# One tile for a chunk's running products and their reciprocals, so that the keys and the queries are each scaled by one VectorE instruction

## The chip, the core and the metric

The kernel runs on one core of a Trainium2 chip, and the metric is the device time in microseconds. Five engines of the core work side by side, each on its own list of instructions in order: TensorE (PE, matrix products; PEld is its loading of weights), VectorE (DVE), ScalarE (ACT), GpSimd (POOL) and SyncE (SP, which here issues nearly all transfers). An engine waits at an instruction until the semaphores of what it needs are set, and everything behind it on that engine waits too.

## The reference, cut to what matters

A linear attention with a decaying state (4 batches, 8 heads, 768 steps, 48 numbers a head) feeds a gated projection and then a mixture of 8 experts of which each row uses 2.

```python
for t in range(S):
    cur = np.einsum('bhd,bhe->bhde', u[None] * kt, vt)
    y[:, :, t] = np.einsum('bhd,bhde->bhe', rt, state + cur)
    state = wt[:, :, :, None] * state + np.einsum('bhd,bhe->bhde', kt, vt)
...
a = x @ w1
b = x @ w2
h = a * b @ w3
x = h @ w_out
...
# two experts of each row, by noisy logits, weights by a softmax over the two
h = np.maximum(x[mask] @ w1[e], 0.0)
out[mask] += top2_w[mask, k, None] * (h @ w2[e])
```

The changed part is the attention. With w the decay of a step, the product of the decays between two steps s < t is what multiplies k at s and r at t.

## The kernel before, in words

The 3072 rows are cut into 24 chunks of 128 steps (six to a batch). A chunk's steps are ordered around its middle: half of them run outwards to the right, half to the left (HC = 64 steps each). `pre_scan` makes, by one scan on VectorE, the running products of w in both directions for 4 pairs of heads (8 runs of 65 numbers, the first of each a 1). `pre_rec` makes their reciprocals: step 0 on ScalarE (exp of minus the log), step 1 one Newton step in two VectorE instructions. `pre_k` scales the keys, `pre_r` the queries: one half of the steps by a running product, the other half by a reciprocal. The products stand in the tile `fg` (two buffers), the reciprocals in `rc` (one buffer), so each half is an instruction of its own with 256 numbers a lane: two for k (L231, L232), two for r (L237, L238). Signs are settled by a factor of -1 inside the two that read `rc`.

The scaled keys and queries `kt` and `rt` go to TensorE (`at_A`, L263: the scores within a chunk). The bonus term needs u·r·k summed over a head: `pre_u` forms it in the tile `rku` (one buffer) from the chunk's `nrk` (r and k by rows, loaded by `load_rk`, two buffers), on VectorE for chunks 2 to 4 and on GpSimd for all others; `pre_c` sums it on VectorE into `cc`; `pre_d` makes eight diagonal tiles `am` from it on ScalarE, and `at_ov` (L268) lays the masked scores over them. `at_y` (L332) then gives the chunk's output, and `at_kv` (L296) the state.

Around the attention stand 19 steps that multiply w3 by w_out while the weights arrive (their conversion, `cvt` and `flush`, keeps VectorE and ScalarE busy: L166, L168, L173), then 12 groups of two chunks of the gated projection (`mo_ab`, `mo_x`), then the experts. The table WHEN sets at which slot each step of chunks 0 to 5 is written into the program, later chunks follow at a fixed distance (6 slots a chunk). VectorE keeps the order of the program throughout, TensorE from the third group on; the other queues are ordered by a scheduler. The buffers matter here: `load_rk(j + 2)` is written right behind `pre_u(j)`, and since `rku` has one buffer, `pre_u` of a chunk on GpSimd waits until the sum `pre_c` of the chunk before has read it. Before the first matmuls, 19 matmuls on a tile `warm` of ones keep TensorE busy.

Of the kernel before, what the change touches and what calls it, by code (L numbers as in the profile page):

```python
# [20 lines left out]
DM, FF, E = 384, 1024, 8  # L21
N = B * S
NCH = N // P
CPB = S // P
NGRP = NCH // 2
HC = P // 2
VW = 64
NDT = 8 * P + 8 * (HC + 1)
NNAT = 2 * DM + H * VW
XW = DM + 16  # L30
TPT, TPL = 128, 32
# [40 lines left out]
def tile_kernel(ctx: ExitStack, tc: tile.TileContext, dt, nat, w3t, wout, w1, w2, e1, e2, cf, ci, out):  # L72
# [8 lines left out]
    class Pinned:  # L81
        on = False
# [5 lines left out]
    act = Pinned()  # L88
# [8 lines left out]
    kdr = nc.dram_tensor("key_halves", [2, 4 * P, 2 * P], U16, kind="Internal").ap()  # L97


    d1 = const.tile([P, 8 * (HC + 1)], F32, name="d1")  # L100
    cft = const.tile([P, CFW], F32, name="cft")
    rounds = const.tile([P, E + 1], I32, name="rounds")
    WAh, WAl, WBh, WBl = [const.tile([P, 8 * XW], F32R, name=n) for n in ("WAh", "WAl", "WBh", "WBl")]
    cit = const.tile([P, CIW], I32, name="cit")

# [78 lines left out]
        pe.matmul(o, wl, xh, start=False, stop=stop)  # L184


    DT, RK, VV, FG, RC, KT, RT, AM, KN, XH, XL, KS = ({} for _ in range(12))

    def load_dt(j):
        DT[j] = att.tile([P, NDT], F32, name="dtc")  # L190
# [2 lines left out]
    def load_rk(j):  # L193
        RK[j] = att.tile([P, 2 * DM], F32, name="nrk")
        sp.dma_start(out=RK[j], in_=nat[j][:, :2 * DM])
# [6 lines left out]
        load_rk(j)  # L202
        load_v(j)

    def fgv(j):
        return FG[j].rearrange("p (a i) -> p a i", i=HC + 1)

    def pre_scan(j):
        FG[j] = att.tile([P, 8 * (HC + 1)], F32, name="fg")
        dve.tensor_tensor_scan(out=FG[j], data0=DT[j][:, 8 * P:], data1=d1, initial=0.0,  # L210
                               op0=OP.mult, op1=OP.add)
        if j % CPB:
            KS["m", j - 1] = att.tile([P, 4], F32, name="sc", bufs=3)
            dve.tensor_tensor(out=KS["m", j - 1], in0=fgv(j - 1)[:, 0::2, HC], in1=fgv(j)[:, 1::2, HC], op=OP.mult)

    def pre_rec(j, step):

        fa = fgv(j)[:, :, 1:]
        if step == 0:
            RC[j] = att.tile([P, 8, HC], F32, name="rc", bufs=1)  # L220
            KT[j] = att.tile([P, 4, 2, HC], F32, name="kt")
            act.activation(out=RC[j], in_=fa, func=AF.Ln)
            act.activation(out=RC[j], in_=RC[j], func=AF.Exp, scale=-1.0)
        else:
            t = KT[j].rearrange("p a s i -> p (a s) i")
            dve.tensor_tensor(out=t, in0=fa, in1=RC[j], op=OP.mult)
# [12 lines left out]

    def pre_u(j):  # L240
        t = att.tile([P, DM], F32, name="rku", bufs=1)
        on = dve if 2 <= j < 5 else pool
        on.tensor_tensor(out=t, in0=RK[j][:, :DM], in1=RK[j][:, DM:], op=OP.mult)  # L243
        on.tensor_tensor(out=t, in0=t, in1=c("u"), op=OP.mult)
        KS["u", j] = t

    def pre_c(j):
        t = KS["u", j]
        cc = att.tile([P, H], F32, name="cc")
        dve.tensor_reduce(out=cc, in_=t.rearrange("p (h d) -> p h d", h=H), axis=mybir.AxisListType.X, op=OP.add)  # L250
# [261 lines left out]
    ld_raw()  # L512
    sp.dma_start(out=cft[:, :ca], in_=cf[:, :ca])
    ld_raw(5)
    warm = fold.tile([P, P], BF16, name="warm", bufs=1)
    dve.memset(warm, 1.0)

    def warm_up(n):
        for _ in range(n):
            tc.keep_in_program_order(pe.matmul(PB[6], warm, warm[:, None, :].to_broadcast([P, 4, P]), start=True, stop=True))  # L520

    warm_up(10)
    for t in TOP:
# [1 line left out]
    for t in St:  # L525
        pool.memset(t, 0.0)
    pool.memset(d1, 0.0)
    pool.memset(d1.rearrange("p (a i) -> p a i", i=HC + 1)[:, :, :1], 1.0)
    pool.memset(zeros, 0.0)
    pool.memset(run, 0.0)  # L530
    pool.memset(oneb, 1.0)

    for u in range(19):
        if u < 8:
# [625 lines left out]
def layout(r, k, v, w, u, moe_w1, moe_w2, moe_w3, moe_w_out, moe2_w_gate, moe2_w_noise, moe2_noise, moe2_w1,  # L1160
# [93 lines left out]
```

## Time and profile before

| what | value |
|---|---|
| three runs, median (lowest to highest) | 884.26 us (883.68 to 884.67) |
| the profiled execution, its own time | 885.03 us |
| its span, first to last instruction | 883.2 us |
| outside the span | 1.8 us |
| granted TensorE clock, mean | 0.999 of full speed |
| PE busy | 868.2 us, 98% of the span |
| DVE busy | 497.3 us, 56% |
| ACT busy | 435.0 us, 49% |
| POOL busy | 243.9 us, 28% |

Busy shares are means over the whole span; the stages differ, so the rows further down go by stretches. Matmuls are pipelined and the ends that the profile gives them are modelled.

### The profile page before, as it was taken

What the parts mean: (1) busy time and instruction counts of PE and PEld (TensorE: products, weight loads), DVE (VectorE), ACT (ScalarE), POOL (GpSimd) and SP (SyncE); (2) the same over time, 40 slices, a digit from 0 to 9 for tenths busy, and PEclk for the clock granted to TensorE, in tenths of its full rate; (3) what the DMA queues carried; (4) which work ended last, traced back from release to release, by engine and by line L of the source; (5) the groups of instructions that cost most, each with busy time, mean ns of one, the idle gap of its engine ahead of it and who ended that gap; (6) DMA issues with size and microseconds to landing.
All of it is one profiled execution on the core that took longest, in us unless ns stands there. A gap on an engine that the chain in (4) does not pass through costs nothing.

```text
span 883.2 us, 18271 instructions
## 1 busy us (share of the span) xinstructions
PE 868.2 (98%) x7333; PEld 808.3 (92%) x7333; DVE 497.3 (56%) x1215; ACT 435.0 (49%) x876; POOL 243.9 (28%) x216
## 2 busy tenths in 40 slices
PE   8999999999999999999999999999999999999996
PEld 6789899999999999999999989899998998989896
DVE  6899875856756756765475453352534434343430
ACT  5777666566466456555454343433433344343431
POOL 2010021041141141232344343407052260613113
PEclk9999999999999999999999999999999999999999
DMA  9955399556467464433266587829368392854213
GB/s 348 390 207 208 97 128 264 134 172 191 118 202 186 133 177 128 98 120 122 69 190 130 157 252 200 210 59 239 84 181 186 93 217 63 242 121 102 27 13 48
DMA packets 123968, 139.22 MB, mean 158 GB/s; under 512 B 74977, under 2 KB 103649, under 8 KB 123873
## 3 DMA queue, kind: packets, MB, share of 16 engines
q1 hardware_dynamic: 100336, 109.58, 43.0%
q0 software_dynamic: 12160, 19.72, 11.6%
q10 hardware_dynamic: 11376, 8.65, 3.0%
q8 instruction: 59, 0.97, 0.5%
q14 instruction: 37, 0.30, 0.1%
HBM read 88.12 MB, written 36.04 MB: 141 GB/s over the span
## 4 chain that ended last, share of the span: by engine, by line
PE 90%; DVE 6%; ACT 2%; issue 1%; DMA 1%; POOL 0%; SPq 0%; POOLq 0%; DVEq 0%; ACTq 0%
PE pb L182 27%; PE pb L183 27%; PE pb L184 26%; PE pb L332 3%; PE pb L263 3%; PE pb L932 1%; PE pb L296 1%; DVE cvz L166 1%; DMA rawf<-wout 1%; DVE w3l L173 1%; ACT top L153 0%; DVE am L268 0%; DVE WAl L173 0%; DVE fg L210 0%; PE pb L412 0%
## 5 line engine op out<-in xcount | busy, mean ns | idle before, releaser
L937 POOL DMA_INDIRECT out<-ye,ti x49 | 76.7, 1565 | 225.3 <-ACT ye L927 204.8
L910 DVE SCALAR_TENSOR_TENSOR HH<-pb,HH 128x256 fp32r<-128x256 f32 (+1 forms) x128 | 71.1, 557 | 112.5 <-ACT HH L909 112.5
L182 PE MATMUL pb<-XTh,WAh 128*128 128x512 f32 (+1 forms) x384 | 131.7, 343 | 0.0
L184 PE MATMUL pb<-XTh,WAl 128*128 128x512 f32 (+1 forms) x384 | 131.4, 342 | 0.0
L183 PE MATMUL pb<-XTl,WAh 128*128 128x512 f32 (+1 forms) x384 | 131.0, 341 | 0.0
L182 PE MATMUL pb<-WBh,HH 128*128 128x384 f32 x384 | 129.3, 337 | 0.0
L184 PE MATMUL pb<-WBh,HH 128*128 128x384 f32 x384 | 128.4, 334 | 0.0
L183 PE MATMUL pb<-WBl,HH 128*128 128x384 f32 x384 | 128.4, 334 | 0.0
L909 ACT ACTIVATE HH<-pb 128x256 fp32r<-128x256 f32 (+1 forms) x128 | 62.7, 491 | 115.6 <-PE pb L184 113.4
L742 POOL DMA_INDIRECT slots<-g_sc,g_si x48 | 51.5, 1073 | 127.5 <-DVE g_si L741 71.9
L927 ACT ACTIVATE ye<-pb,ti 128x384 f32<-128x384 f32 x42 | 24.4, 582 | 124.2 <-PE pb L184 124.2
L183 PE MATMUL pb<-xl,WAh 128*128 128x256 f32 x288 | 80.9, 281 | 0.8 <-DVE xl L339 0.8
L182 PE MATMUL pb<-xh,WAh 128*128 128x256 f32 x288 | 81.5, 284 | 0.0
L183 PE MATMUL pb<-xl,WBh 128*128 128x256 f32 x288 | 81.1, 281 | 0.0
L182 PE MATMUL pb<-xh,WBh 128*128 128x256 f32 x288 | 81.0, 281 | 0.0
L184 PE MATMUL pb<-xh,WBl 128*128 128x256 f32 x288 | 81.0, 281 | 0.0
L184 PE MATMUL pb<-xh,WAl 128*128 128x256 f32 x288 | 80.8, 281 | 0.0
L183 PEld LDWEIGHTS pb<-XTl,WAh 128*128 128x128 f32 x384 | 72.3, 188 | 7.5
L184 PEld LDWEIGHTS pb<-XTh,WAl 128*128 128x128 f32 x384 | 72.2, 188 | 7.5
L182 PEld LDWEIGHTS pb<-XTh,WAh 128*128 128x128 f32 x384 | 72.0, 188 | 7.5
L182 PEld LDWEIGHTS pb<-WBh,HH 128*128 128x128 f32 x384 | 72.1, 188 | 5.0 <-ACT WAh L810 4.4
L243 POOL TENSOR_TENSOR rku<-nrk 128x384 f32<-128x384 f32 x21 | 21.3, 1012 | 196.5 <-DVE cc L250 80.8
(203 smaller groups left out, 2069.1 us busy)
## 6 DMA issues: line engine op xcount, KB each, us to landing
dtc<-dt SPq DMA_DIRECT2D x24, 772.0 KB, 5.1
raw<-e SPq DMA_DIRECT2D x18, 768.0 KB, 6.1
raww<-e SPq DMA_DIRECT2D x14, 768.0 KB, 5.0
nrk<-nat SPq DMA_DIRECT2D x24, 384.0 KB, 5.9
expert_rows<-xg SPq DMA_DIRECT2D x45, 192.0 KB, 4.4
rawf<-w3t SPq DMA_DIRECT2D x16, 512.0 KB, 7.2
nv<-nat SPq DMA_DIRECT2D x24, 256.0 KB, 4.5
out<-zeros SPq DMA_DIRECT2D x9, 576.0 KB, 3.7
```

Of the source, the lines that this page charges most:

```text
L166: dve.scalar_tensor_tensor(z, mid, 13, t, op0=OP.logical_shift_right, op1=OP.bitwise_or)
L182: pin(pe.matmul(o, wh, xh, start=start, stop=False))
L183: pe.matmul(o, wh, xl, start=False, stop=False)
L184: pe.matmul(o, wl, xh, start=False, stop=stop)
L243: on.tensor_tensor(out=t, in0=RK[j][:, :DM], in1=RK[j][:, DM:], op=OP.mult)
L263: pe.matmul(bST[hb][:, P * a:P * a + P], KT[j][q, a].rearrange("p s i -> p (s i)"), RT[j][q, a].rearrange("p s i -> p (s i)"), start=True, ...
L332: pe.matmul(o, lt, rh, start=st, stop=en, tile_position=tp)
L742: ins = pool.indirect_dma_start(out=table, out_offset=bass.IndirectOffsetOnAxis(ap=si[:, i, k:k + 1], axis=0), in_=SC[:, i, k, :], in_offs ...
L909: act.activation(out=Hh[hf][:, ff], in_=bank[:, :n], func=AF.Relu)
L910: dve.scalar_tensor_tensor(Hl[hf][:, ff], bank[:, :n], 0.0, f(Hh[hf][:, ff]), op0=OP.max, op1=OP.subtract)
L927: act.activation(out=y[:n], in_=bank[:n], func=AF.Copy, scale=wt)
L937: ins = pool.indirect_dma_start(out=out, out_offset=bass.IndirectOffsetOnAxis(ap=ti(e, j)[:, 0:1], axis=0), in_=y[:n], in_offset=None, com ...
```

## The change

The running products and the reciprocals of a chunk share one tile `fr` with four blocks of 260 numbers (and a gap of one between blocks): reciprocals of the left runs, left products, right products, reciprocals of the right runs. A block's four runs have 65 numbers each. k's two halves are blocks 1 and 3, r's are blocks 0 and 2, so one strided view gives both halves and each scaling is one instruction of 512 numbers (`times`). The reciprocals start one number earlier in the tile than the products, so that the views line up. The Newton step carries the sign itself, and its two instructions have 520 numbers instead of 512. The input `dt` is laid out by direction, 1545 numbers a lane instead of 1544.

To make room, `rku` goes: `pre_u` writes into its chunk's `nrk`, so the next load into that buffer moves from behind `pre_u` to behind `pre_c`. `rounds` moves into `d1`'s tile, and `warm` becomes `oneb`, which VectorE now fills.

```diff
@@ constants
+FW = 4 * (HC + 1) + 1
-NDT = 8 * P + 8 * (HC + 1)
+NDT = 8 * P + 2 * FW - 1
@@ tile_kernel
-    d1 = const.tile([P, 8 * (HC + 1)], F32, name="d1")
+    d1 = const.tile([P, 2 * FW + E], F32, name="d1")
-    rounds = const.tile([P, E + 1], I32, name="rounds")
+    d1, rounds = d1[:, :2 * FW - 1], d1[:, 2 * FW - 1:].bitcast(I32)
...
-    def fgv(j):
-        return FG[j].rearrange("p (a i) -> p a i", i=HC + 1)
+    def fr(j, o=1):
+        return FR[j][:, o:o + 4 * FW].rearrange("p (b x) -> p b x", b=4)[:, :, :FW - 1]
+
+    def fe(j, b):
+        return fr(j)[:, b].rearrange("p (a i) -> p a i", a=4)
 
     def pre_scan(j):
-        FG[j] = att.tile([P, 8 * (HC + 1)], F32, name="fg")
-        dve.tensor_tensor_scan(out=FG[j], data0=DT[j][:, 8 * P:], data1=d1, initial=0.0,
+        FR[j] = att.tile([P, 4 * FW + 1], F32, name="fr")
+        dve.tensor_tensor_scan(out=FR[j][:, 1 + FW:3 * FW], data0=DT[j][:, 8 * P:], data1=d1, initial=0.0,
                                op0=OP.mult, op1=OP.add)
...
     def pre_rec(j, step):
 
-        fa = fgv(j)[:, :, 1:]
+        fa, rc = fr(j)[:, 1:3], fr(j, 0)[:, 0::3]
         if step == 0:
-            RC[j] = att.tile([P, 8, HC], F32, name="rc", bufs=1)
-            KT[j] = att.tile([P, 4, 2, HC], F32, name="kt")
-            act.activation(out=RC[j], in_=fa, func=AF.Ln)
-            act.activation(out=RC[j], in_=RC[j], func=AF.Exp, scale=-1.0)
+            t = KT["t", j] = att.tile([P, 2, FW - 1], F32, name="kt")
+            KT[j] = t.rearrange("p b x -> p (b x)")[:, :8 * HC].rearrange("p (a s i) -> p a s i", s=2, i=HC)
+            act.activation(out=rc, in_=fa, func=AF.Ln)
+            act.activation(out=rc, in_=rc, func=AF.Exp, scale=-1.0)
         else:
-            t = KT[j].rearrange("p a s i -> p (a s) i")
-            dve.tensor_tensor(out=t, in0=fa, in1=RC[j], op=OP.mult)
-            dve.scalar_tensor_tensor(RC[j], t, -2.0, RC[j], op0=OP.add, op1=OP.mult)
+            t = KT["t", j]
+            dve.scalar_tensor_tensor(t, fa, -1.0, rc, op0=OP.mult, op1=OP.mult)
+            dve.scalar_tensor_tensor(rc, t, 2.0, rc, op0=OP.add, op1=OP.mult)
+
+    def times(out, x, j, b):
+        y = fr(j)[:, b::2].rearrange("p s (a i) -> p a s i", a=4)[:, :, :, :HC]
+        dve.tensor_tensor(out=out, in0=x.rearrange("p (a s i) -> p a s i", s=2, i=HC), in1=y, op=OP.mult)
 
     def pre_k(j):
-        k = DT[j][:, 4 * P:8 * P].rearrange("p (a s i) -> p a s i", s=2, i=HC)
-        dve.tensor_tensor(out=KT[j][:, :, 0], in0=k[:, :, 0], in1=fgv(j)[:, 1::2, :HC], op=OP.mult)
-        dve.scalar_tensor_tensor(KT[j][:, :, 1], k[:, :, 1], -1.0, RC[j][:, 0::2], op0=OP.mult, op1=OP.mult)
+        times(KT[j], DT[j][:, 4 * P:8 * P], j, 1)
 
     def pre_r(j):
         RT[j] = att.tile([P, 4, 2, HC], F32, name="rt")
-        r = DT[j][:, :4 * P].rearrange("p (a s i) -> p a s i", s=2, i=HC)
-        dve.scalar_tensor_tensor(RT[j][:, :, 0], r[:, :, 0], -1.0, RC[j][:, 1::2], op0=OP.mult, op1=OP.mult)
-        dve.tensor_tensor(out=RT[j][:, :, 1], in0=r[:, :, 1], in1=fgv(j)[:, 0::2, :HC], op=OP.mult)
+        times(RT[j], DT[j][:, :4 * P], j, 0)
 
     def pre_u(j):
-        t = att.tile([P, DM], F32, name="rku", bufs=1)
+        t = RK[j][:, :DM]
         on = dve if 2 <= j < 5 else pool
-        on.tensor_tensor(out=t, in0=RK[j][:, :DM], in1=RK[j][:, DM:], op=OP.mult)
+        on.tensor_tensor(out=t, in0=t, in1=RK[j][:, DM:], op=OP.mult)
         on.tensor_tensor(out=t, in0=t, in1=c("u"), op=OP.mult)
...
@@ pre_c
         KS["c", j] = cc
+        if j + 2 < NCH:
+            load_rk(j + 2)
@@ do_u
         pre_u(j)
-        if j + 2 < NCH:
-            load_rk(j + 2)
...
-    warm = fold.tile([P, P], BF16, name="warm", bufs=1)
-    dve.memset(warm, 1.0)
+    dve.memset(oneb, 1.0)
```

On VectorE, here at chunk 4 (`pre_u`, `pre_rec` step 1, `pre_k`, `pre_r`, `pre_c`, then the projection's `pp`), the list before reads:

```order
L243 TENSOR_TENSOR rku<-nrk 128x384
L244 TENSOR_TENSOR rku<-rku,cft 128x384
L226 TENSOR_TENSOR kt<-fg,rc 128x512
L227 SCALAR_TENSOR_TENSOR rc<-kt,rc 128x512
L231 TENSOR_TENSOR kt<-dtc,fg 128x4x64
L232 SCALAR_TENSOR_TENSOR kt<-dtc,rc 128x4x64
L237 SCALAR_TENSOR_TENSOR rt<-dtc,rc 128x4x64
L238 TENSOR_TENSOR rt<-dtc,fg 128x4x64
L250 TENSOR_REDUCE cc<-rku 128x8
```

and after the change:

```order
L250 TENSOR_TENSOR nrk<-nrk 128x384
L251 TENSOR_TENSOR nrk<-nrk,cft 128x384
L233 SCALAR_TENSOR_TENSOR kt<-fr 128x520
L234 SCALAR_TENSOR_TENSOR fr<-kt,fr 128x2x260
L238 TENSOR_TENSOR kt<-dtc,fr 128x512
L238 TENSOR_TENSOR rt<-dtc,fr 128x512
L257 TENSOR_REDUCE cc<-nrk 128x8
```

Nothing changes places; four instructions of 256 numbers became two of 512, in every one of the 24 chunks (VectorE's list is 48 rows shorter).

On SyncE's queue, from the weight loads of the early steps on (`dtc` is a chunk's transposed input, `rawf` a weight block, `nrk` r and k by rows), the list before has the second `nrk` load, that of chunk 2, ahead of chunk 1's:

```order
L191 DMA dtc<-dt 128x1544
L195 DMA nrk<-nat 128x768
L178 DMA rawf<-w3t 128x2048 x2
L178 DMA raw_376<-w 128x3072
L492 DMA cit<-ci 128x166
L178 DMA rawf<-w3t 128x2048 x2
L191 DMA dtc<-dt 128x1544
L195 DMA nrk<-nat 128x768
L199 DMA nv<-nat 128x512
```

and after the change chunk 2's stands behind chunk 1's:

```order
L192 DMA dtc<-dt 128x1545
L179 DMA rawf<-w3t 128x2048 x2
L179 DMA raw_370<-w 128x3072
L499 DMA cit<-ci 128x166
L179 DMA rawf<-w3t 128x2048 x2
L192 DMA dtc<-dt 128x1545
L196 DMA nrk<-nat 128x768
L200 DMA nv<-nat 128x512
L196 DMA nrk<-nat 128x768
```

So one transfer of 384 KB no longer stands ahead of chunk 1's `nrk`.

On ScalarE, around chunk 1's reciprocals (`W0h` is a casting of finished w3·w_out columns, `top` the start of a weight block's conversion, `rc` the log and the exp of chunk 1), the list before reads:

```order
L139 CAST W0h<-pb_75 128x400
L168 CAST w3h<-cvz 128x512
L222 ACTIVATE rc<-fg 128x512
L256 ACTIVATE am<-cft,cc 128x128
L153 ACTIVATE top_111<-rawf 128x512
L223 ACTIVATE rc<-rc 128x512
```

and after the change:

```order
L140 CAST W0h<-pb_72 128x400
L154 ACTIVATE top_110<-rawf 128x512
L169 CAST w3h<-cvz 128x512
L229 ACTIVATE fr<-fr 128x2x260
L154 ACTIVATE top_111<-rawf 128x512
L230 ACTIVATE fr<-fr 128x2x260
```

The conversion `top` moved ahead of the cast, the log and a diagonal tile.

## Rows read from the trace of the kernel before

**Rows 1.** The page, part 1: busy time of each engine, share, instructions.
```profile
PE 868.2 (98%) x7333; PEld 808.3 (92%) x7333; DVE 497.3 (56%) x1215; ACT 435.0 (49%) x876; POOL 243.9 (28%) x216
```

**Rows 2.** Windows: stretch, its length, then each engine's busy time, clock, DMA.
```profile
100.00:120.00 20.00, 18.50 (x263) 16.43 (x263) 17.56 (x37) 11.56 (x27) 2.18 (x3) 1.00 0.36 120
120.00:140.00 20.00, 20.00 (x231) 19.10 (x228) 12.85 (x24) 12.60 (x30) 3.90 (x4) 1.00 1.19 150
```

**Rows 3.** The chain that ended last, in order of time: start, length, what.
```profile
61.00 1.34 DVE am L268 x2
...
110.03 0.42 DVE kt L231
...
111.51 1.16 PE pb L263 x16
```

**Rows 4.** Groups by line and form, VectorE: count, busy us, mean ns of one.
```profile
L227 DVE SCALAR_TENSOR_TENSOR rc<-kt,rc 128x512 f32<-128x512 f32 x24 | 16.6, 692 | 0.8
L226 DVE TENSOR_TENSOR kt<-fg,rc 128x512 f32<-128x512 f32 x24 | 16.3, 681 | 0.0
L231 DVE TENSOR_TENSOR kt<-dtc,fg 128x256 f32<-128x256 f32 x24 | 10.1, 419 | 0.1
```

**Rows 5.** Timeline of VectorE at 63 and 93 us: start, length, instruction.
```profile
62.83 0.68 DVE L173 TENSOR_TENSOR w3l<-cvz,w3h 128x512 fp32r<-128x512 f32 x1
63.43 0.55 DVE L166 SCALAR_TENSOR_TENSOR cvz<-raw,top 128x384 int32<-128x384 int32 x1
...
93.31 0.42 DVE L232 SCALAR_TENSOR_TENSOR kt<-dtc,rc 128x256 f32<-128x256 f32 x1
...
94.31 1.35 DVE L268 COPY_PREDICATED am<-cit,pb 128x512 f32<-128x512 int32 x2
```

**Rows 6.** Timelines of GpSimd, VectorE and TensorE, 44 to 48 us.
```profile
44.42 1.02 POOL L243 TENSOR_TENSOR rku<-nrk 128x384 f32<-128x384 f32 x1 [21.93 <-DMA nrk<-nat]
45.51 1.34 POOL L244 TENSOR_TENSOR rku<-rku,cft 128x384 f32<-128x384 f32 x1
44.42 1.56 DVE L166 SCALAR_TENSOR_TENSOR cvz<-rawf,top 128x512 int32<-128x512 int32 x1 [0.69 <-ACT top L153]
45.91 1.50 DVE L173 TENSOR_TENSOR w3l<-cvz,w3h 128x512 fp32r<-128x512 f32 x1
47.47 0.45 PE L184 MATMUL pb<-WBh,w3l 128*128 128x400 f32 x1 [0.81 <-DVE w3l L173]
```

**Rows 7.** Timelines of GpSimd, SyncE's queue and VectorE, 96 to 112 us.
```profile
112.06 1.01 POOL L243 TENSOR_TENSOR rku<-nrk 128x384 f32<-128x384 f32 x1 [65.20 <-DVE cc L250]
96.12 0.33 SPq L195 DMA_DIRECT2D nrk<-nat  x1
96.72 0.55 DVE L250 TENSOR_REDUCE cc<-rku 128x8 f32<-128x384 f32 x1
101.01 0.36 DVE L304 TENSOR_TENSOR snew<-stmp,sc 128x192 f32<-128x192 f32 x1
103.11 1.23 DVE L210 TENSOR_TENSOR_SCAN fg<-dtc,d 128x520 f32<-128x520 f32 x1
```

**Rows 8.** DMA issues at 96 and 108 us: KB, us from issue to landing.
```profile
nrk<-nat SPq DMA_DIRECT2D x1, 384.0 KB, 5.2
...
nrk<-nat SPq DMA_DIRECT2D x1, 384.0 KB, 3.1
```

**Rows 9.** Timelines of VectorE, TensorE and ScalarE around chunk 5's queries.
```profile
118.88 0.41 DVE L238 TENSOR_TENSOR rt<-dtc,fg 128x256 f32<-128x256 f32 x1
119.52 1.16 PE L263 MATMUL pb<-rt,kt 48*128 48x128 f32 x16
111.16 0.63 ACT L222 ACTIVATE rc<-fg 128x512 f32<-128x512 f32 x1 [1.91 <-DVE rt L237]
```

**Rows 10.** Timelines of VectorE and GpSimd at 166 us.
```profile
165.95 0.69 DVE L589 TENSOR_TENSOR pp<-acs,pb 128x512 f32<-128x512 f32 x1 [0.70 <-PE pb L184]
166.34 1.01 POOL L244 TENSOR_TENSOR rku<-rku,cft 128x384 f32<-128x384 f32 x1
```

More of the change, by code (lines that the diff above doesn't have):

```diff
@@ L184, in mm3 @@
         pe.matmul(o, wl, xh, start=False, stop=stop)
-    DT, RK, VV, FG, RC, KT, RT, AM, KN, XH, XL, KS = ({} for _ in range(12))
+    DT, RK, VV, FR, KT, RT, AM, KN, XH, XL, KS = ({} for _ in range(11))
     def load_dt(j):
@@ L213, in pre_scan @@
             KS["m", j - 1] = att.tile([P, 4], F32, name="sc", bufs=3)
-            dve.tensor_tensor(out=KS["m", j - 1], in0=fgv(j - 1)[:, 0::2, HC], in1=fgv(j)[:, 1::2, HC], op=OP.mult)
+            dve.tensor_tensor(out=KS["m", j - 1], in0=fe(j - 1, 2)[:, :, HC], in1=fe(j, 1)[:, :, HC], op=OP.mult)
     def pre_rec(j, step):
-        fa = fgv(j)[:, :, 1:]
+        fa, rc = fr(j)[:, 1:3], fr(j, 0)[:, 0::3]
         if step == 0:
-            RC[j] = att.tile([P, 8, HC], F32, name="rc", bufs=1)
-            KT[j] = att.tile([P, 4, 2, HC], F32, name="kt")
-            act.activation(out=RC[j], in_=fa, func=AF.Ln)
-            act.activation(out=RC[j], in_=RC[j], func=AF.Exp, scale=-1.0)
-        else:
-            t = KT[j].rearrange("p a s i -> p (a s) i")
-            dve.tensor_tensor(out=t, in0=fa, in1=RC[j], op=OP.mult)
-            dve.scalar_tensor_tensor(RC[j], t, -2.0, RC[j], op0=OP.add, op1=OP.mult)
+            t = KT["t", j] = att.tile([P, 2, FW - 1], F32, name="kt")
+            KT[j] = t.rearrange("p b x -> p (b x)")[:, :8 * HC].rearrange("p (a s i) -> p a s i", s=2, i=HC)
+            act.activation(out=rc, in_=fa, func=AF.Ln)
+            act.activation(out=rc, in_=rc, func=AF.Exp, scale=-1.0)
+        else:
+            t = KT["t", j]
+            dve.scalar_tensor_tensor(t, fa, -1.0, rc, op0=OP.mult, op1=OP.mult)
+            dve.scalar_tensor_tensor(rc, t, 2.0, rc, op0=OP.add, op1=OP.mult)
@@ L514, in tile_kernel @@
     ld_raw(5)
-    warm = fold.tile([P, P], BF16, name="warm", bufs=1)
-    dve.memset(warm, 1.0)
+    dve.memset(oneb, 1.0)
     def warm_up(n):
         for _ in range(n):
-            tc.keep_in_program_order(pe.matmul(PB[6], warm, warm[:, None, :].to_broadcast([P, 4, P]), start=True, stop=True))
+            tc.keep_in_program_order(pe.matmul(PB[6], oneb, oneb[:, None, :].to_broadcast([P, 4, P]), start=True, stop=True))
     warm_up(10)
@@ L527, in tile_kernel @@
     pool.memset(d1, 0.0)
-    pool.memset(d1.rearrange("p (a i) -> p a i", i=HC + 1)[:, :, :1], 1.0)
+    for b in (0, FW):
+        pool.memset(d1[:, b:b + FW - 1].rearrange("p (a i) -> p a i", i=HC + 1)[:, :, :1], 1.0)
     pool.memset(zeros, 0.0)
     pool.memset(run, 0.0)
-    pool.memset(oneb, 1.0)
     for u in range(19):
@@ L1174, in layout @@
     dt[:, :, :D, 4 * P:8 * P] = pairs(kc)[..., TIMES].reshape(NCH, 2, D, 4 * P)
-    fg = dt[..., 8 * P:].reshape(NCH, 2, 64, 4, 2, HC + 1)
+    fg = np.zeros((NCH, 2, 64, 2, 4, HC + 1), np.float32)
     fg[..., 1:] = 1.0
     wp = pairs(wc)
-    fg[:, :, :D, :, 0, 1:] = wp[..., HC:]
-    fg[:, :, :D, :, 1, 1:] = wp[..., HC - 1::-1]
-    dt[..., 8 * P:] = fg.reshape(NCH, 2, 64, 8 * (HC + 1))
+    fg[:, :, :D, 1, :, 1:] = wp[..., HC:]
+    fg[:, :, :D, 0, :, 1:] = wp[..., HC - 1::-1]
+    for b in range(2):
+        dt[..., 8 * P + FW * b:8 * P + FW * b + FW - 1] = fg[:, :, :, b].reshape(NCH, 2, 64, FW - 1)
     nat = np.zeros((NCH, P, NNAT), np.float32)
```

## The prediction, made before the changed kernel was run

> **What bounds the kernel now.** The page's first part comes first: TensorE is busy for 868.2 of 883.2 us, VectorE for 56% [rows 1]. A change that takes work off VectorE can thus pay only where TensorE waits for VectorE, and the windows say where that is. Between 120 and 140 us TensorE is busy for all of 20.00 us and VectorE for 12.85; between 100 and 120 us TensorE has 18.50 and VectorE 17.56, which with some tens of ns between its instructions is full [rows 2]. So there are two regimes: up to about 112 us the kernel waits on VectorE, from then on it is a stream of matmuls whose length the change does not touch. The chain of work says the same: from 61.00 us on its pieces are nearly all VectorE's, ending with chunk 4's keys and queries from 110.03 to 111.51, where TensorE takes over with that chunk's scores [rows 3]. What the change gives or costs is what it moves that last hand-over (111.51 us); everything behind shifts along with it.
>
> **The VectorE instructions.** What counts in a full queue is not an instruction's duration but the step from one start to the next. An instruction with 512 numbers takes 0.68 us, but the next starts after 0.60 (62.83 to 63.43); three steps with 256 numbers take 1.00 (93.31 to 94.31), so 0.33 each [rows 5]. Four of 256 are 1.33 us, two of 512 are 1.20: 0.13 us saved a chunk. (By durations it would be 4 x 419 - 2 x 681 = 314 ns [rows 4]; I do not take that, since neighbours overlap.) The Newton step grows by two times 8 numbers, at (681 - 419) / 256 = 1.02 ns each, 0.02 us, and its first instruction changes to the form of the second, 692 instead of 681 ns [rows 4], 0.01; the scan has one number more, nothing. Net 0.10 us a chunk. The second operand is now read in runs of 64 with a jump between halves; the rows show runs of 64 in both L226 and L231, and both fit one fixed part and 1.02 ns a number, so I take that price unchanged; the bounds are 0.53 a step (512 numbers at 1.02) and 0.67 (two of 256, no gain).
>
> Chunks 2, 3 and 4 lie on the chain: 3 x 0.10 = 0.3 us. Chunks 0 and 1 lie before 61 us, where TensorE, ScalarE and VectorE alternate on the chain: between 0 and 0.2, I take 0.1. Chunks 5 to 23 lie beside a full TensorE and pay nothing; if that cover were gone they would give 1.9. Sum of this part: **-0.4** (0 to -0.7).
>
> ScalarE's log and exp get 8 numbers more and stand beside other work. `oneb` for `warm` is the same fill on VectorE, and one fill less on GpSimd. `rounds` in `d1`'s tile is written long after the last scan. All this I cost at nothing.
>
> **Chunk 1's u·r·k.** At 44.42 us GpSimd starts its two products for chunk 1, when `nrk` lands. VectorE's two instructions of that moment take 1.56 and 1.50 us, and TensorE stands 0.81 us for the second [rows 6]; w3l alone took 0.68 [rows 5]. So a GpSimd product and a VectorE instruction keep each other off. After the change a transfer of 384 KB no longer stands ahead of this `nrk` on SyncE's queue, and ScalarE's `top`, for which VectorE sat idle 0.69 us at 44.42 [rows 6], moves ahead of a cast, the log and a diagonal tile. Both let VectorE be further along. What can be won is TensorE's 0.81; the collision itself does not vanish, it moves by about a microsecond. Bounds 0 and -0.8, I take **-0.4**.
>
> **Chunk 5's u·r·k.** This is the step that speaks against the change. Before, GpSimd held chunk 5's products back until 112.06, 65.20 us of waiting for `cc` of chunk 4, because `rku` had one buffer [rows 7]; by then the hand-over was past. Now they start when chunk 5's `nrk` lands. That load was issued at 96.12, behind VectorE's read for chunk 3; it now waits for `cc` of chunk 3, which ends at 97.27 [rows 7]. From issue to landing it took 5.2 us behind a `dtc`, 3.1 alone [rows 8]. So it lands between 100.4 and 102.5, in the stretch in which VectorE is the bound. The products last 1.0 us each. Landing at 100.4, the first keeps off `snew` (101.01) for 0.4 and the second ends before the scan at 103.11; at 101.3 the second keeps the scan off for 0.3; at 102.5 the first costs the scan 0.4 and the second the next subtraction 0.9. That is 0.3 to 1.3. The bound below is 0 (both meet only what they do not disturb, such as a product that reads a PSUM bank: 0.69 us at 165.95, with GpSimd starting at 166.34 [rows 10]), the bound above two full collisions, 2 x (1.50 - 0.68) = 1.6. I take **+0.6**.
>
> For such pairs the Trainium skill has a rule (SBUF — State Buffer, Who interferes with whom): a VectorE instruction with two operands in SBUF contends with a GpSimd instruction that reads SBUF, whoever starts first holds the port for the whole instruction, and one with at most one operand there does not contend. The rows at 44 and 166 us agree. By that rule the masked copies and the products with a bank between `snew` and the scan would be free and the cost stay near 0.6; by the rows at 44 us alone it could be 1.6.
>
> **Chunk 6's u·r·k** likewise starts earlier: 3.1 to 5.2 us [rows 8] after `cc` of chunk 4, which was there at 112.06 [rows 7], so at 115.2 to 117.3, ahead of chunk 5's queries. There TensorE reaches that chunk's scores at 119.52 and `rt` is ready at 118.88 + 0.41 = 119.29 [rows 9]: 0.23 us to spare. To that comes what a second buffer gives: ScalarE's log for chunk 5 sat 1.91 us until chunk 4's queries had read `rc` [rows 9] and now need not. A single late collision fits, so **0** (0 to +1.0). Later chunks have 7 us of idle VectorE in 20 [rows 2].
>
> Sum: -0.4 - 0.4 + 0.6 + 0 = **-0.2 us**. The profiled execution took 885.03 us, 883.2 of span and 1.8 around it, so it would take 884.8. It lies 0.8 above the median of the runs, 884.26; for that I predict **884.1 us**.
>
> **The rivals.**
> *The gains add up.* `nrk` of chunk 5 meets only instructions that it does not disturb, and chunk 1's stall goes whole: -0.5 - 0.8 = -1.3, so 883.0. For it: between `snew` and the scan VectorE mostly reads banks. Against: the landing has only some 2 us to fall in. Chance 0.17; what the earlier log and `top` may give besides puts about a third of it past -1.8.
> *VectorE is the path throughout.* All 24 chunks pay 0.10: -2.4, so 881.8. Against it stands the full TensorE from 120 us on [rows 2]. Chance 0.07.
> *GpSimd's earlier products cost more than all that is saved.* Freed from waiting for `cc`, they fall into the stretch where VectorE is the bound: chunk 5's with both collisions whole (+1.6), chunk 6's just ahead of chunk 5's queries (+1.0), against -0.4: +2.2, so 886.5. It decides if `nrk` of chunk 5 lands later than about 102 and chunk 6's later than about 116.5. For it: both windows lie within the bounds above. Against: the collisions must both be whole, and the slack of chunk 5's queries has grown. Chance 0.10.
> *The merged products are no cheaper.* A step of 0.67 or more: the first term becomes +0.1, the sum +0.3, 884.6. Nothing in the rows asks for it. Chance 0.06.
>
> **How the numbers follow.** The forecast has 0.60, with a range of its own of 883.0 to 885.2 (its terms between the bounds, not all at one end). A measurement of this kernel can tell about 0.2% from no change, 1.8 us: 882.5 and 886.0. Faster: 0.07 and a third of 0.17, 0.12 to 0.13. Slower: 0.10. The rest, 0.77, is no difference. The range goes from between the first two rivals, 882.3, to short of the third, 885.6, which leaves out the second and most of the third.
>
> **What would show it.** In the new profile: VectorE's products for k and r near 681 ns with 24 each, and VectorE's busy time lower by 24 x (314 - 30) ns, 6.8 us; the GpSimd products of chunk 5 before 104 us instead of at 112; a VectorE instruction of 1 us or more beside them; the hand-over at chunk 4's scores at 111.51 less 0.2, and TensorE without idle time behind 120 us. The prediction is wrong if TensorE shows new waits behind 120 us (a late `nrk` or `dtc`, SyncE's queue stuck behind a load that waits for `cc`), or if the hand-over moves by more than 1.5 us either way.

## The result, and the profile after

The changed kernel took 890.57 us (median of six runs, 887.85 to 891.58) beside 884.0 us (883.68 to 886.3) for the kernel before: ratio 1.0063, 95% interval 1.005 to 1.0075. It is slower, by 6.6 us. The forecast was 884.1 (882.3 to 885.6), with a chance of 0.10 for slower. A repeat in a later series gave 890.01 beside 884.24 us, ratio 1.0066 (1.0044 to 1.0088).

The profiled execution is the fastest of its six (887.85 us, span 886.1): against the profiled execution of before, its trace shows 2.9 us of the loss. First the page's part 1 of the changed kernel, to be laid beside [rows 1]:

```profile
PE 869.4 (98%) x7333; PEld 808.1 (91%) x7333; DVE 506.8 (57%) x1167; ACT 433.4 (49%) x876; POOL 252.6 (29%) x216
```

VectorE has 48 instructions fewer, two a chunk, and is busy 9.5 us longer; GpSimd does the same 216 in 8.7 us more. The groups by line and form of VectorE say which instructions grew [rows 4]:

```profile
L238 DVE TENSOR_TENSOR rt<-dtc,fr 128x512 f32<-128x512 f32 x24 | 18.0, 752 | 0.0
L238 DVE TENSOR_TENSOR kt<-dtc,fr 128x512 f32<-128x512 f32 x24 | 17.3, 719 | 0.1
L221 DVE TENSOR_TENSOR sc<-fr 128x4 f32<-128x4 f32 x20 | 8.5, 427 | 0.8
```

An undisturbed merged product takes 0.68 us, as forecast; the means lie above it, and `sc`, four numbers, has a mean of 427 ns where it took 0.17 undisturbed. The timelines of GpSimd and VectorE in chunk 9's preparation show why:

```profile
169.91 1.52 POOL L250 TENSOR_TENSOR nrk<-nrk 128x384 f32<-128x384 f32 x1 [13.19 <-DMA nrk<-nat]
171.51 1.42 POOL L251 TENSOR_TENSOR nrk<-nrk,cft 128x384 f32<-128x384 f32 x1
169.39 1.24 DVE L217 TENSOR_TENSOR_SCAN fr<-dtc,d 128x521 f32<-128x521 f32 x1
170.66 0.79 DVE L221 TENSOR_TENSOR sc<-fr 128x4 f32<-128x4 f32 x1
171.38 0.68 DVE L608 TENSOR_TENSOR pl<-pp,ph 128x512 fp32r<-128x512 f32 x1
171.98 1.36 DVE L277 COPY_PREDICATED am<-cit,pb 128x512 f32<-128x512 int32 x2
```

GpSimd's products now start when `nrk` lands, just where VectorE has the scan, `sc` and the split (`pl`). Before, `rku`'s one buffer held them back until the sums were read, where VectorE had little to do: GpSimd's first product took 1.01 us in the mean there, and takes 1.23 now.

The windows answer to [rows 2]: TensorE, full in every window between 120 and 800 us before, now has idle time in some. First two windows of before, then the changed kernel:

```profile
160.00:200.00 40.00, 40.00 (x530) 38.78 (x532) 27.57 (x86) 23.04 (x52) 12.74 (x12) 1.00 0.60 170
350.00:400.00 50.00, 50.00 (x616) 48.47 (x615) 35.42 (x105) 27.03 (x59) 14.24 (x14) 1.00 0.38 97
```

```profile
120.00:140.00 20.00, 20.00 (x228) 19.22 (x227) 14.36 (x23) 11.12 (x25) 2.14 (x2) 1.00 1.04 158
160.00:200.00 40.00, 39.85 (x541) 38.17 (x541) 27.16 (x71) 23.71 (x54) 11.95 (x10) 1.00 0.64 165
350.00:400.00 50.00, 49.49 (x604) 47.22 (x602) 37.37 (x99) 26.39 (x59) 13.10 (x11) 1.00 0.40 106
```

Idle time understates it, because a matmul's end is modelled. So I laid the starts of TensorE's 7333 matmuls in the two traces side by side. Between chunk 5's and chunk 23's scores the distance stays the same for tens of us at a time and then jumps, mostly inside one chunk's output products (`at_y`), 56 short matmuls (32 in a sequence's first chunk); the largest jump elsewhere is 0.4 us, near 364 us. Timelines of TensorE and GpSimd, chunk 8:

```profile
180.45 0.55 PE L305 MATMUL pb<-nv,kn 128*32 128x48 f32 x32
180.81 0.40 PE L341 MATMUL pb<-am,nv 128*32 128x128 f32 x8
...
181.15 0.27 PE L341 MATMUL pb<-am,nv 128*32 128x128 f32 x1
181.58 0.29 PE L341 MATMUL pb<-rt,S 128*32 128x128 f32 x1 [0.15 <-issue]
...
182.61 0.47 PE L341 MATMUL pb<-rt,S 128*32 128x128 f32 x5
180.33 0.99 POOL L748 DMA_INDIRECT slots<-g_sc,g_si  x1 [0.30 <-issue]
```

From 180.81 to 182.61 + 0.47 it is 2.26 us, before 1.71: for 0.43 us no matmul starts, and nothing in the trace is waited for. Beside it runs one of GpSimd's eight scatters of a batch of four chunks. A scatter is an indirect transfer: it writes entries of the table `slots`, from which the experts later take their rows, to places that VectorE worked out, and VectorE's cast `g_si` of these places releases it. The same place before:

```profile
179.98 1.00 POOL L243 TENSOR_TENSOR rku<-nrk 128x384 f32<-128x384 f32 x1 [0.18 <-DVE g_si L741]
181.15 1.02 POOL L742 DMA_INDIRECT slots<-g_sc,g_si  x1 [0.16 <-issue]
182.20 1.02 POOL L244 TENSOR_TENSOR rku<-rku,cft 128x384 f32<-128x384 f32 x1
182.49 0.40 PE L332 MATMUL pb<-am,nv 128*32 128x128 f32 x8
...
183.80 0.40 PE L332 MATMUL pb<-rt,S 128*32 128x128 f32 x8
```

There the scatter ends at 182.17, 0.32 us ahead of the output products. Length of the output products in us by chunk, first start to last end, in the traces of the kernels below (the chunks left out are at 1.06 and 1.71 to 1.76, but chunk 0 at 1.79 to 2.16 and chunk 3 at 1.94 to 2.34):

```
                chunk 8    9   12   16   17   20   21   22
before             1.71 1.71 1.06 1.71 1.74 1.71 1.71 1.71
changed            2.26 1.71 1.06 1.98 1.74 2.72 1.75 2.12
changed, repeat    2.29 1.71 1.06 1.98 1.73 2.14 1.71 2.02
e1_hold            1.71 1.78 1.06 1.71 1.74 1.71 1.79 2.01
e2_place_alone     2.31 1.71 1.06 1.89 1.74 2.24 1.71 2.43
e3_u_dve           2.35 1.71 1.06 1.80 1.74 2.24 1.71 2.06
e4_put_later       1.71 6.09 1.06 1.71 3.42 1.71 3.88 1.71
e5_put_in_y        1.71 1.71 1.06 1.71 1.74 1.71 1.71 1.99
e6_sc_later        2.39 1.71 1.06 2.43 1.74 2.28 1.71 1.71
e8_pool_six        2.26 1.71 1.06 1.97 1.74 2.12 1.71 1.77
e9_split_dve       2.63 1.71 1.06 1.91 1.74 2.55 1.71 2.17
e10_put_start      2.90 1.71 2.28 2.91 1.74 2.81 1.71 2.26
e11_put_spread     1.71 1.71 1.06 1.71 1.74 1.71 2.49 1.73
e12_put_six        1.71 1.74 1.06 1.71 1.74 1.71 3.04 1.76
e7_dve_put         1.71 1.71 1.06 1.71 1.74 1.71 1.71 3.77
b1_dve_put         1.71 1.71 1.06 1.71 1.74 1.71 1.71 2.14
```

By stretches, worked out from the starts of the scores (L263 before, L272 in the changed kernel; of chunk 0's, from the first of the twelve that follow each other), from the start of the last matmul and from the end of the span:

```
                chunk 0's scores   0 to 5   5 to 23   23 to last matmul   last matmul to end
before                41.52         78.00    289.75        466.31              7.60
changed               39.85         78.01    292.38        467.08              8.74
changed, repeat       40.19         77.37    292.28        467.31              9.06
e5_put_in_y           40.32         77.22    290.42        467.91              7.77
e10_put_start         40.41         77.17    295.01        467.76              7.66
e1_hold               41.84         77.33    290.18        466.34              7.59
e3_u_dve              40.31         76.73    291.35        466.31              7.41
e8_pool_six           40.81         78.20    291.73        466.32              7.75
e9_split_dve          41.79         77.54    292.19        467.41              7.59
```

The loss lies in two columns: 1.9 to 2.6 us between chunks 5 and 23, and 1.0 to 1.5 us behind the last matmul. The first column is no gain: e5 and e10 are the kernel before up to 176 us, and reach chunk 0's scores at 40.3 to 40.4; the profiled execution of before was a slow one there. Nor does the fourth go with the change: e5, the kernel before with one number moved, has the longest, and e1, e3 and e8 have before's length.

### The profile page after: what moved, and what is told of

It reads as the page before. It is cut to its first block, busy times and chain, and to the rows that moved or that the text cites. A ratio compares the mean times of both kernels' runs of the same rounds, so it can differ in the third digit from the quotient of the medians.

```text
span 886.1 us, 18241 instructions
## 1 busy us (share of the span) xinstructions
PE 869.4 (98%) x7333; PEld 808.1 (91%) x7333; DVE 506.8 (57%) x1167; ACT 433.4 (49%) x876; POOL 252.6 (29%) x216
## 4 chain that ended last, share of the span: by engine, by line
PE 83%; DVE 9%; ACT 4%; DMA 2%; issue 2%; POOL 0%; SPq 0%; ACTq 0%; POOLq 0%; DVEq 0%
PE pb L183 25%; PE pb L184 25%; PE pb L185 25%; PE pb L341 3%; PE pb L272 2%; PE pb L938 1%; ACT am L265 1%; DVE am L277 1%; DMA rawf<-w3t 1%; DVE cvz L167 1%; DVE fr L217 1%; PE pb L305 1%; DMA rawf<-wout 1%; DMA rawf<-w 1%; ACT top L154 1%
## 5 line engine op out<-in xcount | busy, mean ns | idle before, releaser
L250 POOL TENSOR_TENSOR nrk<-nrk 128x384 f32<-128x384 f32 x21 | 25.9, 1233 | 252.0 <-DMA nrk<-nat 185.2
L819 DVE TENSOR_TENSOR WAl<-raww,WAh 128x768 fp32r<-128x768 f32 x28 | 26.7, 957 | 85.8 <-ACT WAh L816 69.8
```

The source lines that it names most:

```text
L250: on.tensor_tensor(out=t, in0=t, in1=RK[j][:, DM:], op=OP.mult)
L819: dve.tensor_tensor(out=l, in0=src, in1=f(h), op=OP.subtract)
```

## The experiments

The theories: A, the products u·r·k that start early stand beside VectorE's instructions and make VectorE late; S, a scatter beside the output products holds TensorE up; T, GpSimd's instructions are fetched in blocks, and the changed number of them puts the edge of a block into the last ones; rival B, the merged tile itself costs.

**e1_hold.** The changed kernel, with GpSimd's products held back as before:

```diff
+        if j > 5:
+            h = att.tile([P, H], F32, name="hold", bufs=1)
+            tc.keep_in_program_order(pool.tensor_copy(out=h, in_=KS["c", j - 1]))
...
```

> The changed kernel, with one addition: from chunk 6 on GpSimd first copies 8 numbers of the sums cc of the chunk before, so that the products u*r*k start when those sums are read, as they did before the change, and not when nrk has landed. Theory A (the products that start early run beside VectorE's instructions, make them longer and put VectorE late against TensorE) expects the loss to go and the gain of the head to stay: 881.5 to 884 us, and the scores and output products of the chunks behind 130 us in step with TensorE. Theory B (the merged tile itself costs: the logarithm now waits for the small product sc, instructions read a strided tile) expects no change against the changed kernel, about 890 us.

885.32 us, ratio to before 1.001 (1.0 to 1.002). Some 5 us of the loss go with one copy of 8 numbers a chunk; the long output products of chunks 8, 16 and 20 go too, and the end is 7.59 us again. (The copies also change the number of GpSimd's instructions, so what the end gives here is not the holding's own; see e8.) The gain of the head that I expected to stay isn't there; in the profiled execution, part of it is lost to a fall of TensorE's clock (last section).

**e2_place_alone.** The kernel before with `t = RK[j][:, :DM]` for `rku` and `load_rk(j + 2)` behind `cc`, nothing merged.

> The kernel before, with only the placing of the change: u*r*k is formed in place in nrk, and the load of nrk for two chunks later is issued behind the sums. Nothing is merged. Theory A expects most of the loss without the gain of the merged instructions: 887 to 892 us. Theory B expects the time of before, 884 us.

890.52 us, ratio 1.0072 (1.0058 to 1.0085): the whole loss, without a merged instruction. As the cause of the loss, B falls.

**e3_u_dve.**

```diff
-        on = dve if 2 <= j < 5 else pool
+        on = dve if j >= 2 else pool
```

> The changed kernel, with the products u*r*k on VectorE for every chunk from 2 on instead of for chunks 2 to 4. GpSimd then reads no SBUF beside VectorE between 60 and 480 us. Two instructions of about 0.5 us more a chunk on VectorE, which is idle 12 of 40 us there. Theory A expects the loss to shrink: 882 to 886 us. Theory B expects 890 us or more, since VectorE gets longer by 1 us a chunk.

885.38 us, 1.0014 (1.0004 to 1.0023). Without GpSimd's products most of the loss goes, as A expects. But chunks 8 and 20 still have long output products: VectorE's casts that release the scatters now stand behind its own u·r·k.

**e4_put_later.** The changed kernel, places of the eight scatters of a batch (in twelfths of a group):

```diff
-                (8, 9, 10, 11, 12, 12, 13, 13) if late else (13, 14, 17, 17, 19, 20, 23, 23))
+                (8, 9, 10, 11, 12, 12, 13, 13) if late else (17, 17, 17, 17, 19, 20, 23, 23))
```

> The changed kernel, with the first two of the eight scatters of slots of a batch of four chunks issued behind the output products of a chunk instead of ahead of them. In the trace of the changed kernel TensorE loses 0.55, 0.27 and 1.01 us inside the output products of chunks 8, 16 and 20, each time with such a scatter on GpSimd beside them. Theory S (the scatter beside the output products is what holds TensorE up there) expects those stalls to go, about 1.8 us: 888.8 us. The rival (VectorE and ScalarE are late there anyway, and the scatter only stands beside it) expects the stalls to stay: 890 to 891 us.

896.56 us, 1.0143 (1.0123 to 1.0163), where 888.8 was expected: slower by 6 us more, and this miss tells the most. Chunks 8, 16 and 20 fall back to 1.71 us, but the scatters, six in a row, now reach the output products of chunks 9, 17 and 21. The last four of them and TensorE at chunk 9:

```profile
196.13 0.96 POOL L748 DMA_INDIRECT slots<-g_sc,g_si  x1 [0.30 <-DVE g_si L747]
197.40 0.96 POOL L748 DMA_INDIRECT slots<-g_sc,g_si  x1 [0.30 <-issue]
198.66 0.96 POOL L748 DMA_INDIRECT slots<-g_sc,g_si  x1 [0.30 <-DVE pp L595]
199.92 0.96 POOL L748 DMA_INDIRECT slots<-g_sc,g_si  x1 [0.30 <-issue]
197.99 0.43 PE L341 MATMUL pb<-am,nv 128*32 128x128 f32 x7
...
198.85 0.41 PE L341 MATMUL pb<-rt,S 128*32 128x128 f32 x3 [0.32 <-issue]
199.57 0.29 PE L341 MATMUL pb<-am,nv 128*32 128x128 f32 x1 [0.30 <-issue]
...
200.29 0.33 PE L341 MATMUL pb<-am,nv 128*32 128x128 f32 x2 [0.29 <-issue]
...
201.72 0.37 PE L341 MATMUL pb<-rt,S 128*32 128x128 f32 x1 [0.99 <-issue]
```

Three scatters beside the output products, five holes of about 0.7 us each from one weight load to the next: 6.09 us instead of 1.71. Some 3 of the 4.4 us are the holes; for the rest, TensorE's clock fell behind them (last section).

**e5_put_in_y and e10_put_start.** The kernel before, one number each: (13, 15.6, 17, 17, 19, 20, 23, 23) and (14, 14, 17, 17, 19, 20, 23, 23).

> The kernel before with one number changed: the cast that releases the second scatter of slots of each batch of four chunks stands behind the next product pp on VectorE, so that this scatter falls beside the output products of chunks 8, 12, 16 and 20 instead of ending 0.3 us ahead of them. Theory S (a scatter on GpSimd beside the output products holds TensorE's issue up) expects 0.5 to 1.0 us more inside each of these output products, 1.5 to 3.5 us in all: 885.7 to 887.7 us. The rival (the scatter only stands beside stalls that lateness of VectorE and ScalarE causes) expects the time of before, 884.2 us, and output products of 1.71 us there.

> The kernel before with one number changed: the first scatter of slots of each batch is released together with the second, so that by GpSimd's order (products, scatter, scatter, products) the second starts about 0.1 us behind the start of the output products of chunks 8, 16 and 20 instead of ending 0.3 us ahead. Theory S in its narrower form (a scatter holds TensorE up when it stands beside the first half of the output products) expects 0.3 to 1.0 us in each of the three: 885.2 to 887 us, and output products longer than 1.9 us there. The rival expects 884.2 us and 1.71 us each.

e5: 885.04 us, 1.0004 (0.9992 to 1.0017), and 1.71 us each (1.06 in chunk 12), although the scatter starts 0.84 us into the output products; in that form S is refuted. Its scatter and the start of the output products at chunk 8:

```profile
181.36 1.02 POOL L742 DMA_INDIRECT slots<-g_sc,g_si  x1 [1.25 <-DVE stmp L303]
180.52 0.40 PE L332 MATMUL pb<-am,nv 128*32 128x128 f32 x8
```

e10: 889.78 us, 1.0052 (1.0035 to 1.007), more than the 887 expected at most: 2.81 to 2.91 us in chunks 8, 16 and 20 and 2.28 instead of 1.06 in chunk 12. Its timelines at chunk 8, GpSimd and TensorE:

```profile
179.20 1.17 POOL L742 DMA_INDIRECT slots<-g_sc,g_si  x1 [0.17 <-issue]
180.67 0.98 POOL L742 DMA_INDIRECT slots<-g_sc,g_si  x1 [0.31 <-issue]
180.55 0.40 PE L332 MATMUL pb<-am,nv 128*32 128x128 f32 x8
...
181.40 0.27 PE L332 MATMUL pb<-am,nv 128*32 128x128 f32 x1
181.98 0.27 PE L332 MATMUL pb<-rt,S 128*32 128x128 f32 x1 [0.31 <-issue]
```

So 5 us come from one number of the kernel before, with nothing of the change in it; the four long output products alone make up 4.7 of them. Over all traces the cost follows the place of the scatter. Where a single scatter ends 0.24 us or more ahead of the output products, they are longer by 0 to 0.09 us; where it ends between 0.04 us ahead and 0.08 us behind their start, by 0.18 to 0.27 (chunk 16 of e2, e8, e9 and the changed kernel); where it ends 0.27 to 0.8 us behind their start, by 0.4 to 0.84; where it starts 0.84 us behind (e5), by nothing. The one exception is chunk 21 of e11, 0.78 us with a scatter that ends as they start: it runs beside the short state products (`at_kv`) just ahead.

**e6_sc_later.** The changed kernel, `sc` of chunks 6 and up moved behind the Newton step.

> The changed kernel, with the small product sc of a chunk's last running products from chunk 6 on behind the Newton step instead of behind the scan, so that ScalarE's logarithm waits for the scan alone, as it did before the change. Theory B (this wait of the shared tile costs) expects part of the loss back: 887 to 889 us. Theory A expects no change: 889.5 to 891.5 us.

889.4 us beside 890.01 for the unchanged one in the same series (six runs each, 888.45 to 891.64 and 887.99 to 892.9). The difference is within the spread, and whether the logarithm's new wait costs a few tenths stays open; the long output products of chunks 8, 16 and 20 are all there (2.39, 2.43, 2.28).

**c1_after.** The changed kernel again.

> The changed kernel once more, for a second trace on the same chip as the other experiments. Every theory expects 889 to 892 us. Theory S expects long output products (over 1.75 us) just where a scatter or gather of GpSimd runs beside them or ends less than 0.3 us ahead.

890.01 us; its rows stand in the tables.

**e7_dve_put and b1_dve_put.** e3_u_dve with the scatters at (17, 17, 17, 17, 23, 23, 23, 23) and at (13, 17, 17, 17, 19, 19, 23, 23).

> The changed kernel with u*r*k on VectorE from chunk 2 on, and with the scatters of slots of a batch in two groups of four, each well behind one chunk's output products and ahead of the next. If the two causes (products on GpSimd beside VectorE, and scatters beside the output products) are the whole of the loss, the gain of the head, 2.6 us at chunk 3, stays to the end: 881.5 to 883.5 us. If something else in the change costs, it stays near the kernel with u*r*k on VectorE alone, 885.4 us.

> The kernel with u*r*k on VectorE and the scatters moved, as e7_dve_put, with the scatters spread over four places, so that those of the last full batch come no later than in the changed kernel and the gathers behind them don't slide into chunk 22's output products, which took 3.76 us in e7_dve_put. Theories A and S expect 2 us less than there: 882.5 to 884 us. If something else costs, it stays at 885 us.

885.03 us, 1.0005 (0.9994 to 1.0016), and 884.86 us, 1.0001 (0.9988 to 1.0013): the time of the kernel before, not better, and above what both expectations gave for the two causes being all. In e7 TensorE keeps in step with the kernel before from chunk 5's scores to chunk 21, and then chunk 22's output products take 3.77 us beside two gathers (indirect reads) that wait for the scatters; b1 has 2.14 there.

**e8_pool_six.** The changed kernel, with `pool.memset(run, 0.0)` seven times instead of once.

> The changed kernel with six more memsets of 128x8 on GpSimd in the head, which repeat one that stands there. In the traces of the changed kernel, of its repeat, of the placing alone and of the one with sc moved, a block of GpSimd's instructions is fetched 1.4 us ahead of the end, and the end lies 3.4 to 3.9 us behind the last packet of the last scatter; in the traces of before and of the five others it is 2.4 us and no such fetch is there. Theory T (the changed number of GpSimd instructions puts a block's edge into its last instructions) expects 2.4 us again with six more instructions, and 1.0 to 1.4 us less in all: 888.7 us. The rival (the late end belongs to the late gate and scatters) expects the long end to stay, 890 us.

888.73 us, 1.0049 (1.0032 to 1.0067). The end comes 7.75 us behind the last matmul instead of 8.74 and 9.06. DMA of the last 3.1 us, the changed kernel and then this one:

```profile
DMA  0000000000000000000004000000000000000000
...
q14 instruction: 1, 0.01, 1.1%
```

```profile
DMA  9823241100000000000000000000000000000000
...
q0 software_dynamic: 39, 0.04, 7.3%
q14 instruction: 2, 0.02, 1.7%
```

In the changed kernel a block of instructions (a packet of the queue `q14 instruction`) comes alone, 1.4 us ahead of the end, when the last data of GpSimd's queue has landed 2 us before; with six instructions more it comes while that data still moves. Of 16 traces, 4 have the late block (the changed kernel, its repeat, e2 and e6): GpSimd has 391 instructions (semaphores counted) in just these, and the last data packet lies 3.4 to 3.9 us ahead of the end. The 12 others have 341, 395 to 398, or 404, and 2.4 to 2.5 us. VectorE's count doesn't sort them: e2 has as many as before, e8 as many as the changed kernel. T holds in both time and trace; that the block is GpSimd's follows from these counts, no row names its engine.

**e9_split_dve.** e3_u_dve unmerged.

> The kernel with u*r*k in place and on VectorE from chunk 2 on, and the load of nrk behind the sums, but with the products and reciprocals as four instructions in tiles of their own, as before the change. Beside e3_u_dve it differs by the merging alone. The prediction's first step (0.4 us gained in the head, nothing later) expects 885.4 to 886.2 us and the scores of chunk 5 about 0.4 us later than there (117.05 us). Theory B (the merged tile costs in every chunk) expects it a us or more faster than e3_u_dve, 884 us or less.

887.86 us, 1.0034 (1.0022 to 1.0047), against 1.0014 for the merged one; 885.4 to 886.2 was expected. From chunk 0's to chunk 5's scores it takes 77.54 us beside 76.73 in e3 (76.71 and 76.67 in e7 and b1): merging is worth 0.8 us in the head. Behind it the unmerged one is slower too, by 0.8 us between chunks 5 and 23, with longer output products in chunks 8 and 20, and by 1.1 us behind chunk 23's scores, a column that doesn't go with the change. So the merged tile costs nothing there.

**e11_put_spread and e12_put_six.** The changed kernel with (13, 17, 17, 17, 19, 23, 23, 23), for the last such batch a 19 in the sixth place, and the same with the six memsets.

> The changed kernel with the scatters of slots at other places alone: the second of a batch moves behind the output products, and the others are spread so that the last ends over a us ahead of the next. The products u*r*k stay on GpSimd beside VectorE. If the scatters are what the products' collisions cost (VectorE late, scatter late, TensorE held up), the long output products of chunks 8, 16 and 20 go, 1.3 to 1.8 us in the traces: 888 to 888.8 us. If the collisions cost by another way too (a later wait of TensorE), stalls show elsewhere and it stays near 890 us.

> The kernel e11_put_spread with the six further memsets on GpSimd. If the two causes add up, 1.0 to 1.4 us less than e11_put_spread: 886.7 to 887.8 us; what then lies above the kernel before (884.2 to 884.7 us) is what the products beside VectorE cost besides the scatters. If the block's edge is worth less in the median than in the trace, it is the same as e11_put_spread.

887.85 us, 1.0043 (1.0028 to 1.0059), and 888.26 us, 1.0041 (1.0024 to 1.0057). The long output products of chunks 8, 16 and 20 are gone; chunk 21 has them instead (2.49 and 3.04), beside scatters. The two can't show T: e11 alone already ends without the late block (398 instructions). Away from chunk 21, e11's waits show something of what the products beside VectorE cost by themselves. TensorE's waits, 120 to 500 us, with the total, how often, and the longest:

```profile
PE pb L341 <- issue: 0.8, 2, 0.4
PE pb L183 <- ACT xh L347: 0.5, 1, 0.5
PE pb L183 <- DVE pp L595: 0.3, 1, 0.3
PE pb L184 <- DVE xl L348: 0.2, 1, 0.2
```

TensorE waits 1.0 us for values that VectorE or ScalarE finished late, and by the starts of its matmuls it loses 2.1 us against the kernel before between 157 and 172 us, with no scatter near. In e12 that is 1.7 us, but in the changed kernel's own two traces 0 and 0.4 us, and 0.2 to 0.4 in e4, e6 and e8. Whether it comes with these places of the scatters or differs by execution isn't separated; 2 us there can't be taken for a part of the changed kernel's loss.

## Why the prediction was wrong

**VectorE's instructions (-0.4).** Right in kind: 0.68 us for each undisturbed merged product, and from chunk 0's to chunk 4's scores 68.29 to 68.34 us in the three merged kernels with u·r·k on VectorE (e3, e7, b1) beside 68.63 in e9, one trace each. That is 0.3 where I had 0.4; 0.5 more comes up to chunk 5's scores, for which I had nothing. But VectorE's busy time, which I had 6.8 us lower, is 9.5 us higher.

**Chunk 1's u·r·k (-0.4).** There was hardly anything to win. The 0.81 us that TensorE waited for `w3l` [rows 6] belongs to that execution alone: e5 and e10, with the same instructions, wait 0.2 us in all between 40 and 60 us, for another value, and both traces of the changed kernel wait 0.3 for `w3l`.

**Chunk 5's u·r·k (+0.6).** Its products started at 97.55, 0.17 us ahead of `snew`, near the early end of my window, and lengthened `snew` from 0.36 [rows 7] to 1.04 us. From chunk 0's to chunk 4's scores it took 69.05 and 68.41 us beside 69.20 and 69.16 in e5 and e10, the same instructions as before, and 69.99 in the profiled execution of before: against e5 and e10 -0.1 to -0.8, and my sum of -0.2 lies within. Two traces of one kernel lie 0.6 apart here, so a sum of this size can't be told from the spread, and its fit is no confirmation of the terms. The hand-over itself came at 108.90 instead of 111.51, further than the 1.5 us that I had named as a sign of error; but with the old instructions it lies at 109.52 and 109.57 in e5 and e10, so most of that is the late start of one execution.

**Chunk 6's u·r·k (0, bounds 0 and +1.0).** The bound above came true. Timelines of GpSimd and VectorE:

```profile
114.34 1.50 POOL L250 TENSOR_TENSOR nrk<-nrk 128x384 f32<-128x384 f32 x1 [14.70 <-DVE LZ L620]
115.92 1.33 POOL L251 TENSOR_TENSOR nrk<-nrk,cft 128x384 f32<-128x384 f32 x1
114.89 1.50 DVE L238 TENSOR_TENSOR kt<-dtc,fr 128x512 f32<-128x512 f32 x1
116.32 1.49 DVE L238 TENSOR_TENSOR rt<-dtc,fr 128x512 f32<-128x512 f32 x1
```

Both products for chunk 5's keys and queries take 1.5 instead of 0.68 us, and from chunk 4's to chunk 5's scores it is 8.96 us, before 8.00. With this the head's sum is +0.2 to +0.8, not -0.2. These rows agree with the rule of the Trainium skill that I cited (SBUF — State Buffer, Who interferes with whom): each instruction waits for the other's whole length, while at 171.98 the masked copies, with one operand in a bank, keep their 0.68 us beside GpSimd.

**The step that failed** is the first, by which only the hand-over at 111.51 us counts: "from then on it is a stream of matmuls whose length the change does not touch", and with it "Later chunks have 7 us of idle VectorE in 20". I took a full TensorE for one that nothing can lengthen, and freed GpSimd's products in 18 more chunks without asking what else is on GpSimd's queue. The stream grew by 1.9 to 2.6 us between chunks 5 and 23 where I had 0. Before, the queue ran scatter, held product, scatter, and the second scatter ended 0.3 us ahead of the output products. Freed, the products are done long before; at chunk 8 VectorE's cast that releases the second scatter comes at 179.37 instead of 179.80, 0.43 us earlier, while TensorE is 1.68 us earlier, and the scatter slides into the output products. e2 shows that the placing alone does it, e1 that holding the products undoes it (both with the effect on the end, next paragraph), e10 that the overlap alone costs such an amount. My third rival had the right sign and the mechanism in chunks 5 and 6 (886.5 us), and no more of it; that it came nearest is in part luck.

**A second cause** no step had: GpSimd's instruction count, 396 before and 391 now, 1.0 to 1.5 us at the end.

**What stays open.** Against the profiled execution of before, the trace shows 2.9 us (3.8 in the two columns named and 0.8 between them, less 1.7 by which before started late); the medians show 5.8 to 6.6. In both series the profiled execution of the changed kernel was the fastest of its six, and so it was in e2, e3, e6 and e8, of 5 to 11, though not in e11 and e12. That is more often than chance would give, so these traces may show a milder execution than most, and what the slower ones lose besides isn't in a trace. How the 6 us divide also stays rough: the block edge about 1.3 (e8 against the repeat, in different series), spreading the scatters about 2 (e11 against the repeat, with the edge in that); that the rest is collisions and scatters at new places is argued, not shown. No version beat the kernel before.

## What to carry to other kernels

A small buffer can be a schedule: before removing one, list what it held back, what then runs on that engine's queue, and beside which stretch of the bounding engine the rest lands. An engine that is busy all the time can still be lengthened: here its stretches of many short instructions were held up, and those of long ones showed nothing. Such stretches are the places to keep another engine's indirect transfers away from. When a change of instruction count moves the very end of a program, look at when the last block of instructions arrives before explaining it with data.

## What the runs showed that I had not expected

- Beside GpSimd's scatters and gathers TensorE's issue stops: in e4 and e10 mostly for 0.66 to 0.72 us from one weight load to the next, the first such hole often being shorter, from 0.41 us on. This is seen only among matmuls that follow each other every 30 ns or so; no such jump shows among the long matmuls. What the two engines share isn't shown.
- After such a hold-up TensorE's clock can fall: in e4 the granted clock is 0.72 over 200 to 206 us, behind output products with holes, and 0.50 from 202 to 204 us, the lower of its two levels (1.2 GHz).
- In 3 of 16 traces (e1, e9, b1) the clock fell at 32 us, after TensorE had stood idle for 0.8 to 0.9 of the 2 us before. Windows of e1_hold:

```profile
30.00:32.00 2.00, 1.09 (x8) 1.12 (x9) 2.00 (x5) 0.99 (x3) 0.00 (x0) 0.98 0.96 377
32.00:34.00 2.00, 2.00 (x7) 1.95 (x7) 2.00 (x5) 1.66 (x3) 0.00 (x0) 0.50 1.05 428
```

  It cost about 1.5 us: by so much TensorE's lead on the kernel before shrank while the clock was low, from 31.9 to 35.3 us; e3, with 1.07 us busy in the same 2 us, kept 1.00. The head's length thus differs between executions by more than the change was to gain.
